# Attention in batches: sums of k on GpSimd, the copy of dilated values ahead of the dilated exponentials, row matmuls behind the other full-array matmuls

## The chip, the cores and the metric

The kernel runs on one core of a Trainium2 chip. The engines are named as in the profile: PE (TensorE, with PEld its weight loads), DVE (VectorE), ACT (ScalarE), POOL (GpSimd) and SP (SyncE, which here issues DMAs). The metric is the device time of one execution in microseconds. The kernel before was timed three times: 841.21, 843.31 and 843.4 us, median 843.31.

## The reference, cut to what matters

Attention over 4 batches, 8 heads, 576 positions and a head dimension of 64 has two branches, which are added. Its result goes through a gated mixture of 8 experts and then through a feed-forward layer. Only attention and the rows handed to the gate are touched here.

```python
q_d = q.reshape(B, H, Sd, factor, D).mean(axis=3)      # factor 4, Sd = 144; k_d, v_d alike
out_d = sm_attn(q_d, k_d, v_d)                          # softmax attention, "dilated"
out_up = np.repeat(out_d, factor, axis=2)
mask = np.abs(pos[:, None] - pos[None, :]) < factor     # local band of 7
scores = np.where(mask, scale * q @ k.T, -1e9)
out_local = softmax(scores) @ v
x = out_up + out_local                                  # rows of 512: 8 heads x 64
logits = x @ w_gate                                     # routing to experts by capacity
...                                                     # experts, then the feed-forward layer
```

## The kernel before, in words

Attention works on 16 pairs of heads (`p`), two heads on the 128 partitions. The local branch of a pair is cut into 9 blocks of 64 positions, and these into three groups of three. Batches `j` of two groups (`BT`, 25 batches) go through a software pipeline. One step of it is called a cycle here: it computes the scores of batch `c` and the transposes and values of batch `c - 2` (`LAG`). A pair has one and a half batches, so three consecutive cycles make a repeating pattern of two pairs.

The steps, with the names that the profile shows:

- Local branch: PE computes the masked scores `sp` (L191, L197). DVE takes their maxima `mxl` (L202) and scales them (L203). ACT computes the exponentials `al`, six a cycle, with their sums `sl` (L210). DVE adds a small number to the sums (L215), takes the reciprocal (L216) and scales `al` (L217). Two cycles later PE transposes `al` into `trl` (L223), ACT copies that to `aT` (L229), and PE multiplies it with v into `pvl` (L240, written pv in the text).
- Dilated branch: POOL adds four neighbouring q into `qdbd` (L106, L109) and four neighbouring v into `v1` (L116, L117; both tiles show as v). DVE adds four neighbouring k into `kd` by one reduction (L121). PE computes the scores `spd` (L136), DVE the maxima `mxd` (L141, L142), ACT the exponentials `ad` (L149), and DVE normalises them (L155 `sd`, L156, L157). PE transposes them into `trd` (L162), DVE copies one half and ACT the other to `adT` (L168), PE multiplies them with `v1` into `opd` (L175), and ACT copies that to `od` (L180).
- DVE adds `pvl` and `od` into `xT` (L254).
- Rows for the gate: PE multiplies a piece of `xT` with an identity beside the gate weights into `rp` (L270, "row matmul"; the two matmuls of one call appear as four instructions in the trace). ACT copies the rows to `xr` (L275), which a DMA stores to DRAM (L286). DVE adds up the gate's part, `lg` (L281) and `L` (L283). There are 36 calls. The first of a cycle uses the one PSUM buffer `rw`; a second one shares the three buffers `tr` with `trl`, `trd` and `opd`.

The order is set by a table of numbers. `emit` gives each step a key, made of the cycle and a fraction; the steps are sorted by key and issued in that order, and `tie` and `pe` keep each engine's queue in the order of issue. Each engine works through its queue in order, so an instruction that waits holds back all behind it. Loads go through SP's queue, sorted the same way. After the last cycle the routing starts, and its first part is already mixed into DVE's queue at the end of attention. The routing's index decides which weights are loaded, and the experts and the feed-forward layer follow.

Of the kernel before, what the change touches and what calls it, by code (L numbers as in the profile page):

```python
# [7 lines left out]
F32 = mybir.dt.float32  # L8
# [6 lines left out]
ALU = mybir.AluOpType  # L15
AX = mybir.AxisListType
# [4 lines left out]
B, H, S, D = 4, 8, 576, 64  # L21
# [9 lines left out]
LAG = 2  # L31
# [23 lines left out]
class Attn:  # L55
# [61 lines left out]
        self.tie('po', G.tensor_tensor(out=v1, in0=v2[:, :, 0], in1=v2[:, :, 1], op=ALU.add))  # L117

    def kdv(self, p):
        kd = self.t[p]['kd'] = self.wk.tile([128, 144], F32, name="kd")  # L120
        self.tie('dv', self.nc.vector.tensor_reduce(out=kd, in_=self.t[p]['k'][:, 3:3 + S].rearrange("p (m r) -> p m r", r=4), op=ALU.add, axis=AX.X))  # L121


    def pe(self, ins):

# [162 lines left out]
    def emit(self, nar=None, rload=None):  # L288
        nc, a = self.nc, self.a
        def masks():  # L290
            nc.sync.dma_start(self.identb, a['identb'])
            nc.sync.dma_start(self.mask.rearrange("p g w -> p (g w)"), a['mask'].rearrange("p g u w -> p (g u w)"))
        def ident():
            nc.sync.dma_start(a['ident_sb'], a['ident'])
        def gate():
            nc.sync.dma_start(a['idg_sb'], a['idg'])
        for i, z in enumerate(self.qdbd):
            (nc.vector if i % 2 == 0 else nc.gpsimd).memset(z, 0.0)
        ops = []
        def add(key, f, *args):  # L300
            ops.append((key, len(ops), f, args))
        nb = len(BT)
        first = lambda p: (3 * p + 1) // 2
        add(-4.7, masks)
        add(-2.5, ident)
        add(1.0, gate)
        add(-4.0, self.busy, FILL0)
        for c, n in FILLC.items():
            add(c + 0.5, self.busy, n)
        for p in range(NP):  # L310
            f = first(p)
            add(1.5 * p - 4.8, self.load, p)
            add(1.5 * p - 2.6, self.load_d, p)
            add(1.5 * p - 1.4, self.load_v, p)
            add(1.5 * p - 2.3, self.prep, p)
            add(1.5 * p + 0.2, self.prep_v, p)
            add(1.5 * p - (1.45 if p != 1 else 0.95), self.kdv, p)
            s = max(f - 1, 0)
            add(s + 0.33, self.spd, p)
            add(s + 0.50, self.mxd, p)  # L320
            add(s + 0.62, self.exd, p)
            add(s + 1.54, self.nmd, p)
            for c in range(2):
                add(s + 2.34 + 0.01 * c, self.trd, p, c)
                add(s + 2.52 + 0.08 * c, self.atd, p, c)
            add(f + LAG + 0.67, self.opd, p)
            add(f + LAG + 1.01, self.odc, p)
        for j in range(nb):
            add(j + 0.00, self.scores, j)
            add(j + 0.04, self.maxes, j)  # L330
            add(j + 0.58, self.exps, j)
            add(j + 1.10, self.norm, j)
            e = j + LAG
            for b in range(len(BT[j])):
                add(e + 0.20 + 0.01 * b, self.trans, j, b)
                add(e + 0.22 + 0.01 * b, self.atc, j, b)
            add(e + 0.70, self.pv, j)
            add(e + 1.02, self.evac, j)
        if rload:
            add(12.0, rload)  # L340
        todo = []
        for t in range(18):
            b, r = divmod(128 * t + 127, S)
            for h in range(2):
                g = 3 * (4 * b + 1 + 2 * h) + r // 192
                k = (g + 1) // 2 + LAG + 1
                todo.append((k + (k < nb + LAG - 1), t, h))
        todo.sort()
        c = 0
        while todo:  # L350
            for n in range(3 if c > nb + LAG - 3 else 2):
                if todo and todo[0][0] <= c and (n == 0 or c % 3 != 1 or c > nb + LAG - 3):
                    _, t, h = todo.pop(0)
                    k = c + (0.30, 0.40, 0.45)[n]
                    if c >= nb + LAG:
                        k = c + 0.04 + 0.1 * n
                    add(k, self.rmm, t, h, n)
                    add(k + (0.15 if c >= nb + LAG - 1 else 0.18 + 0.1 * n), self.rxr, t, h)
                    add(c + 1.06 + 0.01 * n if c < nb + LAG - 1 else k + 0.16, self.rlg, t, h)
                    if h == 1:  # L360
                        add(c + 1.08 if c < nb + LAG - 1 else k + 0.17, self.rst, t)
            c += 1
        for _, _, f, args in sorted(ops):
            f(*args)
# [704 lines left out]
```

## Time and profile before

| | |
|---|---|
| median of three runs | 843.31 us |
| the profiled execution | 837.57 us |
| its span, first to last instruction | 835.8 us |
| busy share of the span: PE, DVE, ACT, POOL | 95%, 80%, 60%, 21% |
| mean granted TensorE clock | 0.995 |

The durations come from the one profiled execution. A busy share is an average over stages that have different limits: attention fills the first 150 us or so, and the experts and the feed-forward layer fill most of the rest. Several instructions that follow each other closely are merged in the timeline, with their count behind an x; the square brackets tell how long the engine had been idle before and what ended that. A wait is put down to the instruction of the other engine that ended last before it.

### The profile page before, as it was taken

The numbers are of one execution on the slowest core, as the hardware profiler recorded it, in microseconds if no ns is written. First come the engines' busy times: TensorE is split into PE (matmuls) and PEld (weight loads), VectorE is DVE, ScalarE is ACT, GpSimd is POOL, SyncE is SP. The second block draws the span as 40 slices with busy tenths as digits, with TensorE's granted clock in tenths as the row PEclk, the third lists the DMA queues.
The fourth block names the chain that finished last, engine by engine and source line by source line (L and its number), as shares of the span: only waits on it lengthen the run. The fifth ranks groups of instructions, "written<-read, shape, count | busy, mean of one in ns | idle before, by whom it ended". The sixth has DMA issues, their size and how long they took to land.

```text
span 835.8 us, 16770 instructions
## 1 busy us (share of the span) xinstructions
PE 795.7 (95%) x6235; PEld 679.2 (81%) x6235; DVE 669.1 (80%) x1699; ACT 497.9 (60%) x1209; POOL 176.0 (21%) x215
## 2 busy tenths in 40 slices
PE   7978888879999999999999999999999999999997
PEld 4877777448998999899998888888878888888886
DVE  6888876768799899999848788888888888657764
ACT  4777777023434444556647777777767777666552
POOL 5654320022121011030000000011223221312223
PEclk9999999999999999999999999999999999999999
DMA  9975532166387496487335434457697674974512
GB/s 240 225 188 180 162 95 102 68 227 223 122 250 253 144 304 238 134 290 276 107 111 183 126 125 128 124 160 199 151 252 175 167 189 103 249 163 128 124 50 76
DMA packets 65106, 142.40 MB, mean 170 GB/s; under 512 B 7968, under 2 KB 20640, under 8 KB 65024
## 3 DMA queue, kind: packets, MB, share of 16 engines
q1 hardware_dynamic: 24704, 70.54, 26.8%
q0 software_dynamic: 29280, 56.63, 26.3%
q10 hardware_dynamic: 11040, 14.16, 4.9%
q8 instruction: 49, 0.80, 0.4%
q14 instruction: 33, 0.27, 0.1%
HBM read 112.98 MB, written 18.88 MB: 158 GB/s over the span
## 4 chain that ended last, share of the span: by engine, by line
PE 66%; issue 8%; DVE 4%; DMA 3%; POOL 2%; ACT 1%; POOLq 0%; SPq 0%; ACTq 0%; DVEq 0%
PE hm L763 6%; PE hm L765 6%; PE hm L764 6%; PE oa L764 6%; PE oa L765 6%; PE oa L763 6%; PE ya L764 4%; PE ya L765 4%; PE ya L763 4%; PE hp L845 4%; PE hp L763 3%; PE hp L764 3%; PE hp L765 3%; PE cnt L522 2%; DMA Yh<-y_dram 1%
## 5 line engine op out<-in xcount | busy, mean ns | idle before, releaser
L763 PE MATMUL hm<-Yh,wM_sb 128*128 128x512 f32 (+1 forms) x320 | 118.5, 370 | 1.6 <-DMA Yh<-y_dram 1.6
L765 PE MATMUL hm<-Yh,wM_sb 128*128 128x512 f32 (+1 forms) x320 | 118.7, 371 | 0.0
L764 PE MATMUL hm<-Yl,wM_sb 128*128 128x512 f32 (+1 forms) x320 | 118.6, 370 | 0.0
L763 PE MATMUL oa<-wM_sb,gh 128*128 128x512 f32 x288 | 113.1, 393 | 0.0
L764 PE MATMUL oa<-wM_sb,gh 128*128 128x512 f32 x288 | 113.1, 393 | 0.0
L765 PE MATMUL oa<-wM_sb,gl 128*128 128x512 f32 x288 | 112.9, 392 | 0.0
L919 DVE SCALAR_TENSOR_TENSOR eu<-eu 128x512 f32<-128x512 f32 x72 | 49.7, 690 | 44.9 <-ACT eu L918 44.6
L763 PE MATMUL ya<-gh,wbh 128*128 128x288 f32 x256 | 79.3, 311 | 1.2 <-DVE Yl L828 1.2
L755 ACT CAST wbh<-wraw 128x512 fp32r<-128x512 f32 x64 | 39.7, 622 | 66.4 <-PE ya L764 37.3
L925 ACT CAST gh<-eu 128x512 fp32r<-128x512 f32 x72 | 44.3, 616 | 54.7 <-DVE eu L922 54.1
L764 PE MATMUL ya<-gl,wbh 128*128 128x288 f32 x256 | 76.4, 299 | 0.2 <-DVE gl L855 0.2
L765 PE MATMUL ya<-gh,wbl 128*128 128x288 f32 x256 | 75.8, 297 | 0.0
L781 POOL DMA_INDIRECT xrow<-x_dram,idx x24 | 32.8, 1366 | 188.8 <-PE ip L623 90.3
L763 PEld LDWEIGHTS hm<-Yh,wM_sb 128*128 128x128 f32 x320 | 60.3, 188 | 13.3 <-DMA Yh<-y_dram 2.3
L926 DVE TENSOR_TENSOR gl<-eu,gh 128x512 fp32r<-128x512 f32 x72 | 49.6, 688 | 25.7 <-ACT gh L925 24.6
L764 PEld LDWEIGHTS hm<-Yl,wM_sb 128*128 128x128 f32 x320 | 60.3, 188 | 11.2
L765 PEld LDWEIGHTS hm<-Yh,wM_sb 128*128 128x128 f32 x320 | 60.2, 188 | 10.7
L914 ACT ACTIVATE eu<-hm 128x512 f32<-128x512 f32 x72 | 42.9, 596 | 40.3 <-PE hm L765 40.1
L763 PEld LDWEIGHTS oa<-wM_sb,gh 128*128 128x128 f32 x288 | 54.0, 188 | 12.8 <-ACT osb L890 0.4
L916 ACT ACTIVATE eu<-eu,one_sb 128x512 f32<-128x512 f32 x72 | 52.1, 724 | 20.6 <-DVE eu L915 19.7
L765 PEld LDWEIGHTS oa<-wM_sb,gl 128*128 128x128 f32 x288 | 54.0, 188 | 12.4
L764 PEld LDWEIGHTS oa<-wM_sb,gh 128*128 128x128 f32 x288 | 54.1, 188 | 11.9
(185 smaller groups left out, 2083.5 us busy)
## 6 DMA issues: line engine op xcount, KB each, us to landing
wraw<-in_wE_dram SPq DMA_DIRECT2D x64, 512.0 KB
n<-in_wM_dram SPq DMA_DIRECT2D x32, 512.0 KB
Yh<-y_dram POOLq DMA_DIRECT2D x16, 1024.0 KB, 9.2
Yl<-y_dram POOLq DMA_DIRECT2D x16, 1024.0 KB, 7.1
part<-osb POOLq DMA_DIRECT2D x36, 256.0 KB, 4.4
vw<-in_vw_dram SPq DMA_DIRECT2D x16, 315.0 KB
kT<-in_kT_dram SPq DMA_DIRECT2D x16, 291.0 KB
qT<-in_qT_dram SPq DMA_DIRECT2D x16, 288.0 KB
```

What stands on the lines that cost most here:

```text
L522: ct = self.behind(nc.tensor.matmul(cnt, cmp[c], OH[:, c], start=(k > 0 and c == 0), stop=(k == 0 and c == 17)))
L755: c = self.nc.scalar.copy(wh, src)
L763: mm(out, lh, rh, start=first, stop=False)
L764: mm(out, lh, rl, start=False, stop=False)
L765: return mm(out, ll, rh, start=False, stop=last)
L781: ld = nc.gpsimd.indirect_dma_start(out=xr, out_offset=None, in_=self.a['x_dram'], in_offset=bass.IndirectOffsetOnAxis(ap=idx[:, g:g + 1], ...
L845: self.r.mm = nc.tensor.matmul(hp, w1[:, 128 * dc:128 * dc + 128], xh[:, dc], start=dc == 0, stop=dc == 3)
L914: nc.scalar.activation(out=e, in_=hp[:, 0:w], func=AF.Exp)
L916: nc.scalar.activation(out=u, in_=e, func=AF.Square, bias=one)
L919: nc.vector.scalar_tensor_tensor(out=u, in0=u, scalar=1.0, in1=r, op0=ALU.add, op1=ALU.mult)
L925: self.cast = nc.scalar.copy(gh[:, 0:w], e)
L926: self.mark = nc.vector.tensor_tensor(out=gl[:, 0:w], in0=e, in1=gh[:, 0:w].bitcast(F32), op=ALU.subtract)
```

## The change

Four things change. The sums of k move from one DVE reduction to two POOL adds, the first over 128x288, the second over 128x144, right behind the q sums of the same pair. The copy `od` is issued with the key of the matmuls that it copies, and the dilated exponentials of all pairs but the first a little later, which puts `od` first on ACT. The copies `adT` of pair 0 are issued earlier. The row matmuls get keys behind `spd` and `trd` and ahead of `opd`, and their copies `xr` keys behind the exponentials.

```diff
--- before.py
+++ after.py
@@ -117,9 +117,12 @@
         self.tie('po', G.tensor_tensor(out=v1, in0=v2[:, :, 0], in1=v2[:, :, 1], op=ALU.add))
 
     def kdv(self, p):
+        G = self.nc.gpsimd
+        k4 = self.t[p]['k'][:, 3:3 + S].rearrange("p (m r) -> p m r", r=4)
+        k2 = self.wk1.tile([128, 144, 2], F32, name="k2")
         kd = self.t[p]['kd'] = self.wk.tile([128, 144], F32, name="kd")
-        self.tie('dv', self.nc.vector.tensor_reduce(out=kd, in_=self.t[p]['k'][:, 3:3 + S].rearrange("p (m r) -> p m r", r=4), op=ALU.add, axis=AX.X))
-
+        self.tie('po', G.tensor_tensor(out=k2, in0=k4[:, :, 0:2], in1=k4[:, :, 2:4], op=ALU.add))
+        self.tie('po', G.tensor_tensor(out=kd, in0=k2[:, :, 0], in1=k2[:, :, 1], op=ALU.add))
 
     def pe(self, ins):
 
@@ -314,17 +317,17 @@
             add(1.5 * p - 1.4, self.load_v, p)
             add(1.5 * p - 2.3, self.prep, p)
             add(1.5 * p + 0.2, self.prep_v, p)
-            add(1.5 * p - (1.45 if p != 1 else 0.95), self.kdv, p)
+            add(1.5 * p - 2.2, self.kdv, p)
             s = max(f - 1, 0)
             add(s + 0.33, self.spd, p)
             add(s + 0.50, self.mxd, p)
-            add(s + 0.62, self.exd, p)
+            add(s + (0.72 if p else 0.62), self.exd, p)
             add(s + 1.54, self.nmd, p)
             for c in range(2):
                 add(s + 2.34 + 0.01 * c, self.trd, p, c)
-                add(s + 2.52 + 0.08 * c, self.atd, p, c)
+                add(s + (2.52 + 0.08 * c if p else 2.36 + 0.08 * c), self.atd, p, c)
             add(f + LAG + 0.67, self.opd, p)
-            add(f + LAG + 1.01, self.odc, p)
+            add(f + LAG + 0.68, self.odc, p)
         for j in range(nb):
             add(j + 0.00, self.scores, j)
             add(j + 0.04, self.maxes, j)
@@ -351,11 +354,11 @@
             for n in range(3 if c > nb + LAG - 3 else 2):
                 if todo and todo[0][0] <= c and (n == 0 or c % 3 != 1 or c > nb + LAG - 3):
                     _, t, h = todo.pop(0)
-                    k = c + (0.30, 0.40, 0.45)[n]
+                    k = c + (0.50, 0.53, 0.56)[n]
                     if c >= nb + LAG:
                         k = c + 0.04 + 0.1 * n
                     add(k, self.rmm, t, h, n)
-                    add(k + (0.15 if c >= nb + LAG - 1 else 0.18 + 0.1 * n), self.rxr, t, h)
+                    add(k + (0.15 if c >= nb + LAG - 1 else 0.10), self.rxr, t, h)
                     add(c + 1.06 + 0.01 * n if c < nb + LAG - 1 else k + 0.16, self.rlg, t, h)
                     if h == 1:
                         add(c + 1.08 if c < nb + LAG - 1 else k + 0.17, self.rst, t)
```

PE's queue, a steady cycle with two row matmuls, from the transposes to the values; before:

```order
L223 MATMUL trl<-ident_sb,al 70x128 x6
L270 MATMUL rp<-idg_sb,xT 128x136 x2
L136 MATMUL spd<-kd,qdbd_154 96x144 x3
L270 MATMUL rp<-idg_sb,xT 128x136 x2
L175 MATMUL opd<-adT,v_1636 64x144 x4
L240 MATMUL pvl<-aT,vw 64x64 x12
```

and now:

```order
L226 MATMUL trl<-ident_sb,al 70x128 x6
L139 MATMUL spd<-kd,qdbd_155 96x144 x3
L273 MATMUL rp<-idg_sb,xT 128x136 x4
L178 MATMUL opd<-adT,v_1350 64x144 x4
L243 MATMUL pvl<-aT,vw 64x64 x12
```

Both calls of the row matmul (two matmuls each) now stand behind `spd`; in cycles with `trd` they stand behind that as well.

ACT's queue, a steady cycle with the copy `adT` and the dilated exponentials; before:

```order
L229 COPY aT<-trl 70x384 x2
L275 COPY xr<-rp 128x256
L210 ACTIVATE al,sl<-sp,mxl 128x70 x6
L168 COPY adT<-trd 72x288
L149 ACTIVATE ad,sd<-spd,mxd 96x144 x3
L180 COPY od<-opd 128x144
```

and now:

```order
L232 COPY aT<-trl 70x384 x2
L213 ACTIVATE al,sl<-sp,mxl 128x70 x6
L171 COPY adT<-trd 72x288
L278 COPY xr<-rp 128x256
L183 COPY od<-opd 128x144
L152 ACTIVATE ad,sd<-spd,mxd 96x144 x3
```

The copy `xr` went from ahead of the six exponentials `al` to behind them and `adT`, and `od` from behind the three exponentials `ad` to ahead of them.

DVE's queue, a steady cycle without `spd`, from the sums `xT` to the copy `adT`; before:

```order
L254 TENSOR_TENSOR xT<-pvl,od 128x192 x2
L202 TENSOR_REDUCE mxl<-sp 128x6
L203 TENSOR_SCALAR mxl<-mxl 128x6
L121 TENSOR_REDUCE kd<-kT 128x144
L281 TENSOR_REDUCE lg<-rp 128x8
L215 TENSOR_SCALAR sl<-sl 128x6
L216 RECIPROCAL sl<-sl 128x6
L217 TENSOR_TENSOR al<-al,sl 128x420
L168 COPY adT<-trd 72x288
```

and now:

```order
L257 TENSOR_TENSOR xT<-pvl,od 128x192 x2
L205 TENSOR_REDUCE mxl<-sp 128x6
L206 TENSOR_SCALAR mxl<-mxl 128x6
L284 TENSOR_REDUCE lg<-rp 128x8
L218 TENSOR_SCALAR sl<-sl 128x6
L219 RECIPROCAL sl<-sl 128x6
L220 TENSOR_TENSOR al<-al,sl 128x420
L171 COPY adT<-trd 72x288
```

The reduction `kd` between the scaled maxima and `lg` is gone; all else stands as it stood. At the end of attention one more thing moves on DVE: the first large compare of the routing, `cmp` (L438), now stands behind the next `xT`, two `lg` and one `sl`. On SP's queue the routing's four tables are issued two pairs of loads later.

## Rows read from the trace of the kernel before

**Rows 1.** Table by stretches, steady part: us, busy per engine (instructions), granted clock, DMA share, GB/s.
```profile
25.79:140.60 114.81, 97.32 (x1595) 86.06 (x1591) 94.11 (x276) 86.14 (x430) 44.88 (x61) 1.00 0.56 163
25.79:34.07 8.28, 8.28 (x154) 7.67 (x150) 7.36 (x19) 6.79 (x35) 5.58 (x7) 1.00 0.91 232
```

**Rows 2.** Waits, 25.79 to 140.6: engine line waited for, us in total, times, longest.
```profile
ACT xr L275 <- PE rp L270: 19.2, 18, 1.7
PE rp L270 <- DVE lg L281: 12.7, 16, 1.5
DVE xT L254 <- ACT od L180: 11.1, 12, 1.8
POOL qdbd L109 <- PE spd L136: 10.4, 6, 2.4
PE rp L270 <- DVE sl L215: 3.4, 2, 1.9
```

**Rows 3.** Timeline of PE, three cycles: start, us long, instruction [idle before it].
```profile
72.32 0.70 PE L270 MATMUL rp<-idg_sb,xT 128*128 128x136 f32 x4 [1.54 <-DVE lg L281]
72.86 0.66 PE L162 MATMUL trd<-ident_sb,ad 96*72 96x96 f32 x6
...
76.96 0.73 PE L270 MATMUL rp<-idg_sb,xT 128*128 128x136 f32 x4 [0.29 <-DVE lg L281]
...
82.96 0.73 PE L270 MATMUL rp<-idg_sb,xT 128*128 128x136 f32 x4 [0.89 <-DVE lg L281]
83.53 0.90 PE L136 MATMUL spd<-kd,qdbd 128*96 128x144 f32 x6
```

**Rows 4.** Timeline of DVE, same cycles.
```profile
71.35 0.74 DVE L121 TENSOR_REDUCE kd<-kT 128x144 f32<-128x576 f32 x1
...
81.47 0.56 DVE L254 TENSOR_TENSOR xT<-pvl,od 128x384 f32<-128x384 f32 x1 [0.95 <-ACT od L180]
```

**Rows 5.** Groups by line, 25.79 to 140.6: shapes xcount, busy us, mean ns, idle before.
```profile
L157 DVE TENSOR_TENSOR ad<-ad,sd 96x432 f32<-96x432 f32 x14 | 10.7, 766 | 0.5
...
L121 DVE TENSOR_REDUCE kd<-kT 128x144 f32<-128x576 f32 x12 | 8.9, 740 | 0.0
...
L203 DVE TENSOR_SCALAR mxl<-mxl 128x6 f32<-128x6 f32 (+1 forms) x21 | 5.5, 260 | 0.7
...
L109 POOL TENSOR_TENSOR qdbd<-q 64x144 f32<-64x144 f32 x22 | 9.5, 432 | 11.5 <-PE spd L136 10.4
...
L106 POOL TENSOR_TENSOR q<-qT 128x288 f32<-128x288 f32 x11 | 8.7, 794 | 0.0
```

**Rows 6.** The scalings of the maxima and of `ad`, 25.79 to 140.6: duration ns min/median/max.
```profile
L203 DVE TENSOR_SCALAR mxl<-mxl x21: 169/172/1027, 27.7 to 137.7; 128x6 f32<-128x6 f32 x20, 128x3 f32<-128x3 f32 x1
...
L157 DVE TENSOR_TENSOR ad<-ad,sd x14: 604/605/1509, 26.1 to 135.3; 96x432 f32<-96x432 f32 x14
```

**Rows 7.** Timeline of POOL and DVE, a v add beside a scaling.
```profile
73.86 1.27 POOL L116 TENSOR_TENSOR v<-vd 72x512 f32<-72x512 f32 x1 [5.18 <-DMA vd<-in_vd_dram]
74.08 1.51 DVE L157 TENSOR_TENSOR ad<-ad,sd 96x432 f32<-96x432 f32 x1
```

**Rows 8.** Timeline of DVE and PE, the first dilated output.
```profile
18.60 0.45 DVE L168 COPY adT<-trd 72x288 f32<-72x288 f32 x1
...
19.19 1.23 PE L175 MATMUL opd<-adT,v 72*64 72x144 f32 x8 [2.61 <-DVE sd L155]
```

**Rows 9.** Table by stretches, 16 to 24 us.
```profile
16.00:20.00 4.00, 1.39 (x15) 1.21 (x15) 3.79 (x10) 3.22 (x19) 3.26 (x5) 0.71 0.95 219
20.00:24.00 4.00, 4.00 (x50) 3.60 (x47) 1.32 (x4) 0.56 (x3) 3.40 (x5) 0.50 0.95 266
```

**Rows 10.** Timeline of DVE and PE, end of attention.
```profile
140.50 1.02 DVE L438 TENSOR_TENSOR cmp<-E,rthr 128x1664 f16<-128x1664 bf16 x1
...
142.12 1.66 PE L270 MATMUL rp<-idg_sb,xT 128*128 128x136 f32 x12 [0.67 <-DVE lg L281]
```

**Rows 11.** Chain that ended last, last gate sum: start, us, what.
```profile
150.53 0.18 DVE L L283
```

## The prediction

> **What bounds the kernel now.** I read the chain of waits first. Attention ends with the last gate sum, at 150.53 us [rows 11]; the chain goes straight on from it into the routing, then the weight loads, the experts and the feed-forward part, all of which need the routing. Nothing later hides a microsecond that attention gives back, so I count gains ahead of 150.53 us one to one.
>
> Then I read the table by stretches for the steady part, 25.79 to 140.60 us [rows 1]. Of 114.81 us PE is busy 97.32, DVE 94.11, ACT 86.14, POOL 44.88. No engine is full, but PE is nearest. The waits of that stretch say what stops it: the row matmuls `rp` wait for DVE's `lg` and, by the order in which DVE ends, `sl`: 12.7 + 3.4 = 16.1 us [rows 2]. PE's whole idle time is 114.81 - 97.32 = 17.5 us, so this one wait is nine tenths of it. `rp` needs the PSUM buffer that `lg` of the cycle before still reads, and `lg` stands on DVE behind `xT`, the maxima and, in some cycles, `kd`. Two more waits belong to it: ACT's `xr` waits 19.2 us for `rp`, with the exponentials queued behind it, and DVE's `xT` waits 11.1 us for ACT's `od`, with `mxl` and `lg` queued behind that.
>
> The timeline shows three consecutive cycles, the pattern that repeats: `rp` waits 1.54, 0.29 and 0.89 us, together 2.72 [rows 3]. In the first, `kd` runs 0.74 us just ahead of `lg`; in the third, `xT` stood 0.95 us for `od` [rows 4].
>
> **The change part by part.** *Row matmuls behind the other full-array work (PE).* In the first kind of cycle `rp` now follows the `trd` transposes (0.66 us), in the second `spd` and `trd` (0.90 + 0.66), in the third `spd` (0.90) [rows 3]. That work fills the time in which `lg` is awaited. In the first cycle 0.66 from the order and 0.74 from the missing `kd` cover 1.40 of 1.54; in the second 1.56 covers 0.29; in the third 0.90 covers 0.89. Left: about 0.14 of 2.72 us. On the PE side the 16.1 us go almost wholly. What is late next is ACT or DVE.
>
> *Copies and exponentials (ACT).* `xr` moves behind the six exponentials, so these no longer stand behind a copy that waits for PE; `od` moves ahead of the three dilated exponentials, so `xT` no longer waits for them. ACT's own work stays at 86.14 us. New: DVE's `sd` now waits for ACT itself, because `od`, for which `xT` waits, no longer comes after `ad`. Behind `sd` stand its reciprocal, the scaling of `ad` and the next `xT`. `ad` now ends behind one or two copies `xr` and the copy `od`, but `sd` comes a cycle after it; I count nothing, and a late `sd` would show as a wait of DVE for `ad`.
>
> *Sums of k (DVE to POOL).* DVE loses 16 reductions of 0.740 us, 11.8 us in all, 8.9 in the stretch. POOL gains 16 pairs of adds. The first has the shape of the q add, 128x288, 0.794 us. The second, 128x144, is not in the trace: its elements per partition are those of `qdbd`, 0.432 us, and it cannot well cost more than the first, 0.794 [rows 5]. I take 0.432, the row with the same length per partition, and keep the other end: 16 x 1.226 = 19.6 us, at most 16 x 1.588 = 25.4. POOL has room: it waits 10.4 us for PE's `spd` before `qdbd` [rows 2], which means that it runs ahead by its three buffers, and in the stretch it is busy 45 of 115 us. Behind the new adds on POOL's queue stand only the v sums and the next q sums. I count no wait of PE for `kd`; if POOL lost its lead, each late pair would cost PE up to the 1.23 us of the two adds.
>
> What it does cost is DVE. Where POOL's `v` add runs from 73.86 for 1.27 us, DVE's scaling of `ad` beside it takes 1.51 us [rows 7], against 0.604 at its fastest; over the stretch its mean is 0.766, and that of the scaling of the maxima 0.260 against a median of 0.172 [rows 5, 6]. So 14 x (0.766 - 0.605) + 21 x (0.260 - 0.172) = 4.1 us of DVE time are lost beside 44.88 us of POOL, 9%. The other small DVE operations lose too; I take double, 18%, an estimate. The stretch gets about 11.5 new pairs, 14 us of POOL, so 2.5 us of new DVE stall. DVE's load there goes from 94.1 to 94.1 - 8.9 + 2.5 = 87.7 us.
>
> The Trainium skill speaks against this part: "SBUF — State Buffer", section "Who interferes with whom", says that VectorE and GpSimd share one port pair as an exclusive lock, that a VectorE instruction with two SBUF inputs blocks against a GpSimd one that reads SBUF, and that a reduction never contends. By it the change swaps a harmless instruction for blocking ones; the trace agrees on the block (1.51 against 0.604 us [rows 6, 7]) and shows it for 9% of the POOL time, 18% by my estimate. By the rule at its worst, all added POOL time stops DVE; that result is the last rival below.
>
> *How much of the 16.1 us comes back.* From 25.79 to 34.07 us no row matmul runs yet. There PE is busy 8.28 of 8.28 us, with DVE at 89%, ACT at 82% and POOL at 67% [rows 1]: this pipeline can run with PE never waiting. After the change DVE wants 87.7 us and ACT 86.1 where PE wants 97.3, so 90% and 88%. For DVE that is what the rows show, for ACT more. If ACT can't pass 82%, the stretch takes 86.14 / 0.82 = 105.1 us, 9.7 saved; if PE sets the pace alone, 16.1 are saved. I take 11.3, three tenths of the waits left, nearer to the end that a row shows.
>
> *Start and end.* The first `opd` waits 2.61 us, and the copies it needs stand behind other work, on DVE at 18.60 us [rows 8]; the diff puts that copy earlier on ACT and `kd` is off DVE's queue. Between 0 and 2.6; I take 0.7, the one `kd`. From 16 to 20 us PE is busy 1.39 us and the granted clock falls to 0.71; from 20 to 24 us PE is fully busy at 0.50, the 1.2 GHz level [rows 9]; if the clock no longer fell, half of those 4 us would come back, which I leave to the range. At the end DVE's first large compare, 1.02 us at 140.50, now stands behind `xT` and two `lg`; behind it today PE's `rp` waits 0.67 us [rows 10]. I take 0.5, between 0 and 0.67. The routing's four small tables load two pairs later on SP's queue; they are used only at the end of attention, so nothing.
>
> **Sum.** 11.3 + 0.7 + 0.5 = 12.5 us. The profiled execution took 837.57 us with a span of 835.8, and should become 825.1. It was 5.7 us below the median of the runs shown, 843.31; on that basis I forecast 830.8 us. Its own range is a gain of 8 to 16 us, 827 to 835.
>
> **The rivals.** *PE sets the pace alone.* For it: the wait-free stretch [rows 1]. Against: ACT at 88% has no row. 16.1 + 2.6 + 0.67, perhaps 2.0 for the clock: 16 to 21 us, about 824. Chance 0.12; the forecast has 0.58.
>
> *ACT takes the place of the wait.* `xr`, `od` and `ad` end later in the cycle, so the next copies `aT` start late and `pv` waits for them. At a share of 79% the stretch takes 109.0 us: 5.8 saved, with start and end 7.0; at 77%, 111.9 us, 2.9 saved, 4.1 with them. Gains of 2.5 to 8 us, so about 838. Chance 0.17. For it: ACT never passed 82%. Against: its waits for `rp`, 19.2 us [rows 2], are what goes.
>
> *The wait only moves,* from `rp` to `trl`, `opd` or `pv`, and nothing is gained: 843. Little speaks for it, since `lg` itself comes earlier. Chance 0.06.
>
> *DVE blocked by POOL: slower.* If POOL's added 19.6 us all stopped DVE, DVE would have 19.6 - 11.8 = 7.8 us more, and with the longer pair 13.6; DVE would then hold `lg` back as it does now and set the pace: 851 us, up to 857. It decides from the point where more than 11.8 / 19.6 = 60% of the added POOL time blocks DVE. The rows show 9 to 18%, and the stretch with POOL at 67% had no PE wait. Chance 0.07. The Trainium skill, "SBUF — State Buffer", section "Who interferes with whom", describes this lock.
>
> **How the numbers follow.** About 0.3%, 2.5 us, is what a measurement of this kernel can tell from no change. Faster: 0.58 + 0.12 + 0.17 = 0.87. Same: 0.06. Slower: 0.07. The range reaches from the rival in which PE sets the pace, 824, to most of the one in which ACT does, 840; beyond it lie the last two and a little at the fast end, under 2 in 10.
>
> **What would show it.** Attention's last gate sum near 138 us instead of 150.53. PE's wait for `lg` under 5 us in the steady part, no wait of ACT's `xr` for `rp`, `xT` no longer waiting for `od`. Means of DVE's scalings above 0.766 and 0.260 while POOL works, and the second add on POOL near 0.43 us. I am wrong if the `rp` wait stays over 8 us, if PE waits as long at `pv` or `trl` instead, or if DVE's scalings lose more than 7 us in all.

## The result and the profile after

The changed kernel took 831.0 us (median of four runs, 825.8 to 833.6) where the kernel before took 842.3 beside it: 0.985 of the time, 95% interval 0.981 to 0.989. That is 11.3 us less; 12.5 were forecast, and 830.8 us. Two later comparisons, on two different chips, gave 826.1 against 842.9 (0.981, 0.978 to 0.984) and 826.6 against 842.6 (0.982, 0.978 to 0.986): gains of 16.8 and 16.0 us. The three intervals overlap, but the later gains are those of the rival "PE sets the pace alone".

The first profiled execution of the changed kernel took 831.68 us with a span of 829.9 us; that of the kernel before took 837.57 us with 835.8. The wait that the change aimed at is gone. Waits of the steady part after, 25.79 to 140.6 us (us in total, times, longest), to be read against [rows 2]:

```profile
...
ACT aT L232 <- PE trl L226: 14.1, 18, 3.2
...
ACT aT L232 <- DMA vd<-in_vd_dram: 5.1, 1, 5.1
DVE mxl L205 <- PE sp L200: 4.4, 9, 1.3
PE trd L165 <- ACT aT L232: 4.2, 3, 2.6
DVE xT L257 <- ACT ad L152: 3.5, 1, 3.5
...
ACT xr L278 <- PE rp L273: 2.6, 4, 1.3
...
PE trd L165 <- DVE lg L284: 2.0, 4, 0.7
DVE xT L257 <- ACT od L183: 1.3, 2, 0.7
...
PE rp L273 <- DVE lg L284: 1.0, 2, 0.5
```

PE's `rp` waits 1.0 us for `lg` instead of 12.7, ACT's `xr` 2.6 instead of 19.2, DVE's `xT` 1.3 for `od` instead of 11.1. What grew is waiting for PE: ACT's `aT` for `trl`, 14.1 us instead of 7.0, and DVE's `mxl` for `sp`, 4.4 instead of 1.0. The three single waits of 5.1, 2.6 and 3.5 us are new; they are one event, below. The timeline of PE shows how `rp` now stands behind `spd` and `trd` (start, us, instruction [idle before it]); compare [rows 3]:

```profile
81.19 0.90 PE L139 MATMUL spd<-kd,qdbd 128*96 128x144 f32 x6
81.92 1.09 PE L273 MATMUL rp<-idg_sb,xT 128*128 128x136 f32 x8
...
86.46 0.69 PE L165 MATMUL trd<-ident_sb,ad 96*72 96x96 f32 x6 [0.29 <-ACT aT L232]
86.99 1.12 PE L273 MATMUL rp<-idg_sb,xT 128*128 128x136 f32 x8
...
91.99 0.69 PE L165 MATMUL trd<-ident_sb,ad 96*72 96x96 f32 x6 [0.48 <-DVE lg L284]
92.51 0.66 PE L273 MATMUL rp<-idg_sb,xT 128*128 128x136 f32 x4
```

No `rp` waits in these three cycles. A little of the wait moved to `trd`, 0.77 us where `rp` had waited 2.72. The table by stretches after (us, then busy us of PE, PEld, DVE, ACT, POOL, the granted clock, DMA share, GB/s), of the whole stretch of [rows 1], of eleven cycles in its second half, and of one cycle ahead of them:

```profile
25.79:140.60 114.81, 105.41 (x1659) 94.04 (x1658) 95.83 (x284) 87.90 (x434) 62.85 (x89) 0.97 0.67 177
74.59:127.19 52.60, 50.72 (x855) 46.24 (x852) 45.16 (x136) 45.04 (x229) 24.95 (x36) 1.00 0.52 152
53.11:63.44 10.33, 7.09 (x86) 6.19 (x83) 6.76 (x16) 5.07 (x26) 8.55 (x14) 0.79 0.90 236
```

From 74.59 us on PE is busy 50.72 of 52.60 us, 96%, with ACT and DVE at 86%. But the one cycle from 53.11 to 63.44 takes 10.33 us, and PE is busy in 7.09 of them although the clock stands at 0.79. The timelines of ACT and of PE there:

```profile
53.16 0.66 ACT L278 COPY xr<-rp 128x256 f32<-128x256 f32 x2
54.63 4.21 ACTq L289 DMA_DIRECT2D x_dram<-xr  x2
58.89 0.85 ACT L232 COPY aT<-trl 70x384 f32<-70x384 f32 x2 [5.07 <-DMA vd<-in_vd_dram]
```

```profile
56.42 0.44 PE L165 MATMUL trd<-ident_sb,ad 96*72 96x96 f32 x3 [0.69 <-DVE lg L284]
59.41 0.70 PE L165 MATMUL trd<-ident_sb,ad 96*72 96x96 f32 x3 [2.56 <-ACT aT L232]
```

ACT's queue takes 4.21 us to issue the first two row stores, until a `vd` load lands, and ACT is idle for 5.07 us; behind the stores stands `aT`, and PE waits for that. Before the change the same two issues took 0.35 and 0.34 us:

```profile
57.49 0.35 ACTq L286 DMA_DIRECT2D x_dram<-xr  x1
...
59.19 0.34 ACTq L286 DMA_DIRECT2D x_dram<-xr  x1
```

PE's idle time is followed by a granted clock of 0.50, the 1.2 GHz level, from 60 to 66 us. The order of the built kernel says why a store waits for a load. In it the transfers of SP and ACT take turns on eight semaphores, DMAHW0 to 7, and each waits until the one before it on its own semaphore is complete. After the change the first two stores have numbers 2 and 4. Eight places ahead of them on these numbers stand a `kT` and a `vd` load, which SP issued at 41.57 and 45.84 us; before, the stores' predecessors were the small tables `rthr` and `rtri`:

```
35 L90 DMA kT_833<-in_kT_dram 128x582 [waits DMAHW2_49]
37 L94 DMA vd_910<-in_vd_dram 72x1024 [waits DMAHW4_49,Pool_49]
...
68 L289 DMA x_dram_57<-xr_780 128x512 [waits DMAHW2_49,Activation_49]
69 L289 DMA x_dram_57<-xr_782 128x512 [waits DMAHW4_49,Activation_49]
```

Attention's last gate sum starts at 140.28 us instead of 150.53 [rows 11], 10.2 us earlier, while the span is 5.9 us shorter:

```profile
140.28 0.17 DVE L286 SCALAR_TENSOR_TENSOR L<-lg 128x8 f32<-128x8 f32 x1
```

What follows attention took 689.6 us, against 685.3 before. Over the fourteen traces of this case it took 684.2 to 690.6, in code that the change doesn't touch.

### The profile page after: what moved, and what is told of

Same layout as the page of the kernel before. It is cut to its first block, busy times and chain, and to the rows that moved or that the text cites. A ratio compares the mean times of both kernels' runs of the same rounds, so it can differ in the third digit from the quotient of the medians.

```text
span 829.9 us, 16780 instructions
## 1 busy us (share of the span) xinstructions
PE 798.7 (96%) x6235; PEld 682.1 (82%) x6235; DVE 666.5 (80%) x1683; ACT 495.9 (60%) x1209; POOL 195.6 (24%) x247
## 4 chain that ended last, share of the span: by engine, by line
PE 73%; DMA 11%; issue 8%; DVE 4%; POOL 2%; ACT 1%; SPq 0%; POOLq 0%; ACTq 0%; DVEq 0%
PE hm L768 7%; PE hm L767 7%; PE hm L766 7%; PE oa L766 6%; PE oa L767 6%; PE oa L768 6%; DMA vd<-in_vd_dram 5%; PE ya L767 4%; PE ya L768 4%; PE ya L766 4%; PE hp L848 3%; PE hp L766 3%; PE hp L768 3%; PE hp L767 3%; PE cnt L525 2%
## 5 line engine op out<-in xcount | busy, mean ns | idle before, releaser
L922 DVE SCALAR_TENSOR_TENSOR eu<-eu 128x512 f32<-128x512 f32 x72 | 49.7, 690 | 45.0 <-ACT eu L921 44.7
L767 PEld LDWEIGHTS hm<-Yl,wM_sb 128*128 128x128 f32 x320 | 60.6, 189 | 11.3
L894 POOL DMA_DIRECT2D part<-osb x36 | 33.2, 1014 | 138.0 <-ACT osb L893 112.0
L766 PEld LDWEIGHTS oa<-wM_sb,gh 128*128 128x128 f32 x288 | 54.1, 188 | 12.8 <-ACT osb L893 0.4
```

What stands on the lines that cost most here:

```text
L766: mm(out, lh, rh, start=first, stop=False)
L767: mm(out, lh, rl, start=False, stop=False)
L894: nc.gpsimd.dma_start(p, o, accum_op=ALU.add)
L922: nc.vector.scalar_tensor_tensor(out=u, in0=u, scalar=1.0, in1=r, op0=ALU.add, op1=ALU.mult)
```

## The experiments

All ran beside the kernel before, in three comparisons; the numbers are medians of six runs, those of the kernel before of eleven. Each kernel has one trace, and the last three columns come from it. One measure is used throughout, from the timeline of PE: how long nine cycles take, from the start of the 5th cycle's scores to the 14th's (first half, where the changed kernel's loads keep the DMA engines about 90% busy) and from the 14th's to the 23rd's (second half).

| kernel | ratio to before, 95% | first half, us | second half, us | last gate sum, us |
|---|---|---|---|---|
| before | 1 | 49.0 | 51.1 | 150.5 |
| changed, three traces | 0.985, 0.981, 0.982 | 50.6, 44.1, 44.9 | 43.6, 43.6, 45.2 | 140.3, 134.5, 135.8 |
| row matmuls alone | 0.991 (0.988 to 0.994) | 46.7 | 46.0 | 141.1 |
| copies alone | 0.992 (0.989 to 0.994) | 50.0 | 48.7 | 148.0 |
| sums of k alone | 0.993 (0.990 to 0.995) | 49.9 | 49.7 | 150.0 |
| without sums of k | 0.986 (0.983 to 0.989) | 47.1 | 44.9 | 137.6 |
| tables early | 0.980 (0.978 to 0.983) | 47.1 | 44.2 | 136.1 |
| tables early, without sums of k | 0.983 (0.980 to 0.986) | 45.7 | 45.4 | 136.7 |
| sums of k doubled | 0.986 (0.983 to 0.988) | 45.0 | 45.3 | 141.9 |
| late stores | 0.982 (0.978 to 0.986) | 43.7 | 46.0 | 136.7 |
| first three sums on DVE | 0.980 (0.976 to 0.984) | 43.7 | 43.8 | 133.8 |
| both | 0.982 (0.978 to 0.986) | 44.7 | 46.7 | 138.3 |

In each of the three single parts the routing's tables move as well, though no edit names them: SP issues `rthr` at 60.60, 66.58 and 55.40 us in the traces of the row matmuls, the copies and the sums, and at 44.23 in the kernel before. None of the three is its part alone, then. What the later tables do in the kernel before was not tried; in the changed kernel, early tables leave the time as it is (below).

**Row matmuls alone.** The kernel before with

```
-                    k = c + (0.30, 0.40, 0.45)[n]
+                    k = c + (0.50, 0.53, 0.56)[n]
-                    add(k + (0.15 if ... else 0.18 + 0.1 * n), self.rxr, t, h)
+                    add(k + (0.15 if ... else 0.10), self.rxr, t, h)
```

> The kernel before with only the row matmuls and their copies xr moved to the end of the full-array part; kd stays on DVE, od stays behind the dilated exponentials. Theory (all three parts cure one and the same wait, PE's rp behind DVE's lg, 16.1 us, so alone each gives less than its share and the three together less than their sum would be): by the rows of the three cycles the moved work fills 0.66 + 0.29 + 0.90 = 1.85 of 2.72 us, 68%, so 11 us of the wait at most, less what DVE then still loses to kd and od: a gain of 6 to 9 us against before, PE's wait for lg down to 4 to 8 us, DVE's xT still waiting about 10 us for ACT's od. Rival (the row matmuls do everything): a gain of 10 to 13 us, the same as the whole change. Rival (without kd and od moved, xT only becomes later and the wait moves to trl or pv): a gain of 0 to 2 us.

Measured: 833.5 against 841.1 us, 7.6 less. Waits, 25.79 to 140.6 us:

```profile
...
DVE xT L254 <- ACT od L180: 7.6, 11, 1.6
PE rp L270 <- DVE lg L281: 4.9, 8, 1.0
...
ACT xr L275 <- PE rp L270: 2.5, 4, 1.3
```

The theory's gain and its wait for `lg` hold; `xT` waited 7.6 us for `od` rather than about 10. By the last gate sum, one trace of each kernel, this part brings 9.5 us, where the whole change brings 10.2, 16.0 and 14.7 in its three traces, the copies 2.5 and the sums 0.5. By the medians the three parts are not told apart (7.6, 6.6 and 5.5 us), and together they are more than the whole.

**Copies alone.** The kernel before with

```
-            add(s + 0.62, self.exd, p)
+            add(s + (0.72 if p else 0.62), self.exd, p)
-            add(f + LAG + 1.01, self.odc, p)
+            add(f + LAG + 0.68, self.odc, p)
```

and the first pair's `adT` copies earlier, as in the change.

> The kernel before with only od moved ahead of the dilated exponentials (and the first pair's dilated copies earlier). Theory: xT's wait for od, 11.1 us in the steady part, goes; lg stands behind xT, so lg comes earlier in the cycles in which od was waited for, one in three or so with 0.95 us, and PE's wait for lg falls by 3 to 5 us; a gain of 3 to 5 us. Rival (the row matmuls do everything): 0 to 1 us. Rival (od ahead of ad makes ad late, sd waits): 0 to 3 us slower, with DVE waiting for ad at sd.

Measured: 834.5 us, 6.6 less; more than expected by the medians. The trace bears out half of the reason:

```profile
...
ACT xr L275 <- PE rp L270: 14.1, 17, 1.7
...
PE rp L270 <- DVE lg L281: 11.9, 18, 1.7
...
DVE xT L254 <- ACT od L180: 1.4, 2, 0.8
```

`xT` hardly waits for `od` any more, but PE still waits 11.9 us for `lg` where a fall by 3 to 5 was expected; the last gate sum is only 2.5 us earlier. Part of that is a hold-up in this trace too: ACT is idle 2.80 and 2.74 us at row stores, and the cycle from 62.05 takes 7.9 us.

```profile
59.80 0.85 ACT L229 COPY aT<-trl 70x384 f32<-70x384 f32 x2 [2.80 <-PE spd L136]
...
67.01 0.85 ACT L229 COPY aT<-trl 70x384 f32<-70x384 f32 x2 [2.74 <-PE rp L270]
```

The traced execution of the kernel before was 3.5 to 5.3 us below the medians of that kernel, so a trace set against it shows less than the medians do, and where the rest of the 6.6 us lies isn't shown.

**Sums of k alone.** The kernel before with the new `kdv` and its key.

> The kernel before with only the sums of k moved to GpSimd. Theory: kd, 0.74 us, no longer stands ahead of lg in two of three cycles; in the stretch that is 8.9 us less DVE work, of which about half stands in the time in which PE waits: a gain of 3 to 6 us, POOL busy 19.6 us more, means of DVE's scalings up by under 0.1 us. Rival (DVE blocked by GpSimd): no gain or up to 5 us slower, with the scalings' means up by 0.2 us or more. Rival (the row matmuls do everything): 0 to 1 us.

Measured: 835.5 us, 5.5 less, with the same reserve; the last gate sum is 0.5 us earlier.

```profile
...
DVE xT L257 <- ACT od L183: 13.4, 13, 1.8
PE rp L273 <- DVE lg L284: 12.8, 16, 1.5
```

In the trace the missing reductions only let DVE wait longer for `od`, 13.4 instead of 11.1 us, and PE waits for `lg` as before; where the 5.5 us of the medians lie, it doesn't show. GpSimd did not slow the kernel.

**Without the sums of k.** The changed kernel with the old `kdv` and its key.

> The changed kernel with the sums of k back on DVE at their old place in the order. Theory: with the row matmuls behind spd and trd, PE waits little for lg even with kd on DVE, but DVE's load returns to about 94 us in a stretch of 105, nearly full, so 2 to 5 us slower than the changed kernel, still 6 to 10 us faster than before; DVE busy over 92% in the steady part. Rival (GpSimd's adds cost DVE more than the reduction did): up to 3 us faster than the changed kernel. Rival (kd is off every path): within 1 us of the changed kernel. The hold-up of ACT's queue at the first row stores, 4.2 us in the changed kernel, should be there in this one too, since the routing tables stand equally late on SP's queue.

Measured: 828.3 against 841.1 us, 12.8 less; from this comparison alone, no different from the changed kernel. The hold-up of ACT's queue, expected here too, did not come: the two issues took 0.83 us, not 4.2. DVE was busy 46.4 of 52 us from 70 us on, 89%, not over 92. The next comparison, with the changed kernel in it, is the better test of the sums.

**The changed kernel again.** No edit.

> The changed kernel once more, unaltered, as the measure for the next three and for a second trace. Theory (ACT's queue stands at the issue of the first two row stores, because each of them waits for the completion of an older load that is still under way, and behind it stand aT, xr and ad): the hold-up appears again near 54 us, for 3 to 5 us, one cycle of the scores lasts 9 to 11 us, and the granted clock falls to 0.50 behind it; 829 to 832 us. Rival (the hold-up of the first trace was an accident of one execution, not of the order): all cycles from 25 to 120 us under 6.5 us, time nearer to 826.

Measured: 826.1 against 842.9 us. In this execution the rival holds: no cycle from 25 to 120 us is over 6.3 us. Line of ACT's queue at the first two stores, then its table row from 73.97 to 123 us:

```profile
52.96 0.83 ACTq L289 DMA_DIRECT2D x_dram<-xr  x2
```

```profile
73.97:123.00 49.03, 47.23 (x795) 43.02 (x791) 42.01 (x133) 42.03 (x214) 20.04 (x27) 1.00 0.46 138
```

The 0.83 us are the two issues one behind the other, and ACT's next copy then waits for PE. So the hold-up is not in every execution: the issues took 4.21, 0.83 and, in a third trace, 2.36 us. The order makes it possible; that the speed of the loads ahead decides it fits the first trace, where the `vd` load lands 12.7 us after its issue, but was not tried. Without it the first half takes 44.1 us instead of 50.6.

**Tables early.** The changed kernel with

```
-            add(12.0, rload)
+            add(8.0, rload)
```

> The changed kernel with the routing's four small tables loaded earlier (before the seventh pair's v rows instead of after the tenth pair's k), nothing else. The first two row stores then wait for small tables that landed long before, instead of a k load and a v load just issued. Theory (the store's wait holds ACT): the issue at the first stores takes under 1 us, no cycle over 7 us there, the clock stays at 1.00 from 25 us on; attention's last gate sum 3 to 5 us earlier than in the changed kernel; 3 to 6 us faster than it, about 826. Rival (the loads themselves set the pace up to 65 us, and the store only shows it): the late cycle stays, with aT or v1 or qdbd waiting for a load, and the time within 1.5 us of the changed kernel.

Measured: 826.1 us, the same as the changed kernel in that comparison; the trace still has a cycle of 9.1 us, from 50.30. ACT stands 5.0 us ahead of `aT`, and the profile's view of the table `rthr` names `aT` as what waited for it.

```profile
56.03 0.85 ACT L232 COPY aT<-trl 70x384 f32<-70x384 f32 x2 [5.01 <-issue]
```

The tables `rsmall` and `rthr`, which stand ahead of the two stores on their semaphores here, were issued at 44.82 and 46.43 us and had not landed when the stores came near 51; SP had issued its vd load just ahead at 43.06, into DMA engines that are 91% busy from 25 to 50 us. So my edit had exchanged one late predecessor for another, and the premise "landed long before" was false.

**Tables early, without the sums of k.** The last edit and that of the variant without the sums, together.

> The changed kernel with the tables earlier and with the sums of k back on DVE. Theory (the store's wait accounts for what the sums of k seemed to cost): since the variant without the sums on GpSimd had a hold-up of only 0.83 us, earlier tables give it under 1.5 us; with the tables early, the sums on GpSimd are worth 0 to 3 us, so this one is 0 to 3 us slower than the changed kernel with early tables. Rival (GpSimd's adds cost DVE more than the reduction did): this one is the fastest of all, 2 us or more faster than the changed kernel with early tables.

Measured: 828.7 us, 2.5 more than with the sums on GpSimd in the same comparison. That is as the theory has it (0 to 3), against the rival, and at the edge of what can be told apart.

**Sums of k doubled.** The changed kernel with each add issued twice:

```
-        self.tie('po', G.tensor_tensor(out=k2, ...))
+        for _ in range(2):
+            self.tie('po', G.tensor_tensor(out=k2, ...))
```

and the same for `kd`.

> The changed kernel with each of the two adds of k issued twice on GpSimd (the same result written twice): POOL's work up by another 17.4 us (16 times 0.665 + 0.425). Theory (a tenth to a fifth of POOL's time stops DVE, and DVE has room): 1.7 to 3.5 us more DVE time, of which under half shows, 0 to 2 us slower than the changed kernel; means of DVE's scalings up by less than 0.1 us. Rival (POOL's time blocks DVE one to one): 8 us slower or more, DVE busy over 95% of the steady part. A second rival is POOL's own lead: up to about 55 us POOL is busy three quarters of the time, and with 1.1 us more for each pair PE waits there at spd for kd, 3 to 6 us in all.

Measured: 830.6 us, 4.5 more than the changed kernel. The cycles take no longer (45.0 and 45.3 us); the loss is at the start, where the second rival put it, though before 24 us rather than up to 55:

```profile
18.94 1.75 PE L141 MATMUL spd<-kd,qdbd 128*96 128x144 f32 x6 [3.01 <-POOL kd L127]
```

The fourth cycle's scores start at 23.61 us, in the changed kernel of the same comparison at 19.17. Summed over DVE's groups up to the last gate sum, DVE was busy 125.2 us, against 123.1, 121.5 and 118.5 in the three traces of the changed kernel: 4.2 us more than their mean, for 19.9 us more of POOL, 21%. The three traces differ among themselves by 4.6 us, so the share is rough; but POOL does not block DVE one to one.

**Once more, and three variants.** The last comparison was about the two losses seen.

> The changed kernel, unaltered, as the measure for the next three. Theory (in the steady part PE alone sets the pace; now and then an execution loses 4 to 5 us near 54 us where ACT's queue stands at a row store behind a load that lands late): 825 to 831 us, 12 to 17 us less than before. Rival (the first comparison, 11.3 us, is the typical one): 830 to 833 us.

Measured: 826.6 against 842.6 us. The first two stores took 2.36 us, but the larger loss came later, at the fourth store:

```profile
64.60 0.85 ACT L232 COPY aT<-trl 70x384 f32<-70x384 f32 x2 [1.92 <-DMA kT<-in_kT_dram]
```

ACT was idle 1.92 us until a `kT` load landed, PE waited 2.23 us at `trd`, the granted clock was 0.50 from 66 to 72 us, and the cycles from 60.42 and 68.43 took 8.0 and 6.9 us.

Late stores:

```
-                        add(c + 1.08 if c < nb + LAG - 1 else k + 0.17, self.rst, t)
+                        add(min(c + 4.08, nb + LAG + 0.08) if c < nb + LAG - 1 else k + 0.17, self.rst, t)
```

with the stores tied into ACT's order. In this order the tables `rthr` and `rtri` stand ahead of the first two stores again, as in the kernel before, so both the time of the stores and what they wait for have changed.

> The changed kernel with the row stores of the steady part three cycles later in ACT's order, near 68 us and after, where the loads are through; nothing else. Theory (the store's wait on an older transfer holds ACT only while the load queue is full): no hold-up of ACT's queue over 1.5 us between 50 and 70 us, no cycle over 7 us there, and the spread of the times smaller; the median 0 to 3 us below the changed kernel's in the same comparison. Rival (the loads themselves set the pace there): a cycle of 8 us or more stays, with another wait for a load, and the time is within 1 us.

```profile
67.01 0.35 ACTq L289 DMA_DIRECT2D x_dram<-xr  x1
67.46 0.40 ACTq L289 DMA_DIRECT2D x_dram<-xr  x1
```

In this trace there is no hold-up and no cycle between 50 and 70 us is over 5.3 us, with the same loads under way. That speaks for the store as what held ACT and against the rival (the loads set the pace); but the changed kernel's second trace had no hold-up either, and the last variant below, with the same late stores, had one. And the time, 828.3 us, is not below the changed kernel's 826.6. The first half is the shortest with one other, 43.7 us; the second half, 46.0, is longer than in the changed kernel. Why isn't settled.

The first three sums of k on DVE, with their old keys:

```
+        if p < 3:
+            kd = ...; self.tie('dv', self.nc.vector.tensor_reduce(out=kd, ...)); return
```

> The changed kernel with the sums of k of the first three pairs on DVE again, at their old place; the other thirteen stay on GpSimd. Theory (at the start GpSimd has no lead, and PE waits 1.2 to 1.9 us at spd for its kd): that wait falls to 1.0 us or less, the fourth cycle of the scores starts 0.5 to 1.5 us earlier unless the granted clock falls otherwise; 0 to 2 us faster than the changed kernel. Rival (DVE is the engine at its limit at the start): opd waits again 1 to 2.6 us for DVE, as before the change, and the time is the same or up to 1.5 us more.

Measured: 825.1 us, the lowest median of all, 1.5 below the changed kernel beside it and inside the scatter of either (822.0 to 828.9 and 822.3 to 830.2). PE no longer waits for `kd` at the start, but `opd` waits 1.5 us for DVE's `adT`: theory and rival each hold for one wait, and the fourth cycle starts no earlier (19.47 us; 19.89, 19.17 and 19.19 in the changed kernel).

> The changed kernel with both: row stores three cycles later and the first three sums of k on DVE. Theory: the two act in different places, so their gains add: 0 to 5 us below the changed kernel in the same comparison, 824 to 826 us if both hold. Rival: no measurable difference from the changed kernel, within 1.5 us.

Measured: 828.2 us, 1.6 us more than the changed kernel beside it and inside the scatter; the gains of the theory are not there. Its first two stores, at 71 us, were held again, this time behind the table `rtri`, which SP had issued at 65.09 us; ACT was idle 3.3 us, and the cycle from 68.14 took 6.8 us (line of the waits: us in total, times, longest):

```profile
ACT aT L236 <- DMA rtri<-in_rtri_dram: 3.3, 1, 3.3
```

No version is shown to beat the changed kernel.

## Why the prediction was right, and where not

The time, 830.8, was met at first and lies 4.7 and 4.2 us above the later two medians; the direction and the place, the `rp` wait and the last gate sum (near 138; 140.3, 134.5 and 135.8), were right. By its steps:

- **Row matmuls behind `spd` and `trd`: right.** [rows 3] left about 0.14 of 2.72 us by the sum; `rp` waits none and `trd` 0.77 in three cycles after. The row matmuls alone gave 7.6 us by medians.
- **How much of the 16.1 us comes back: the term that was mis-sized.** I left three tenths, because ACT had no row above 82%. After, PE is busy 96% with ACT and DVE at 86%: the bound read from one stretch of 8.28 us [rows 1] was no bound. From the 5th cycle to the last gate sum the traces took 124.7 us before, and 109.9 in the execution without a hold-up: 14.9 less, nine tenths of the 16.1. In the first, 116.3, 8.5 less. That the first comparison met the forecast is luck: the 11.3 us that I took lie between these two; the pipeline does better than I gave it, and in the first execution it lost about 6.5 us in its first half again.
- **The tables on SP's queue, "nothing": failed.** Their move changed what the first row stores wait for, and in the first trace ACT was idle 5.07 us by it. I had looked at when the tables are used, not at what their place in the count of semaphores does. How much of the difference between 11.3 and 16.8 us it explains isn't settled: moving the tables did not lower the time, nor did the stores' later place, and both moves still had a hold-up in a trace (5.0 and 3.3 us) when what the store waited for had not landed.
- **`od` ahead of `ad`: right as a whole.** `xT`'s wait for `od` went from 11.1 to 1.3 us; it waited once, 3.5 us, for `ad` in the held-up cycle, and not at all in the other two traces. No wait for a late `sd` shows.
- **Sums of k: the costs right.** POOL's busy time rose from 176.0 to 195.6 us, the 19.6 forecast. The second add was put near 0.43 us, and DVE's scalings were to go above 0.766 and 0.260 [rows 5]:

```profile
L124 POOL TENSOR_TENSOR k<-kT 128x288 f32<-128x288 f32 x12 | 8.6, 713 | 0.9
L125 POOL TENSOR_TENSOR kd<-k 128x144 f32<-128x144 f32 x12 | 5.8, 484 | 0.9
```

```profile
L160 DVE TENSOR_TENSOR ad<-ad,sd 96x432 f32<-96x432 f32 x14 | 10.9, 780 | 0.5
...
L206 DVE TENSOR_SCALAR mxl<-mxl 128x6 f32<-128x6 f32 (+1 forms) x21 | 6.0, 285 | 0.7
```

  (Groups after: busy us, mean ns, idle before.) The share of POOL's time that stops DVE, put at 18%: with the sums alone DVE's busy time to the last gate sum is 120.5 us, where 127.3 less 16 x 0.740 would be 115.5, so 5.0 of 19.6 us or 26%; in the changed kernel against the two without the sums it is 16%, doubled 21%. These shares are rough: traces with the same work on DVE differ by 2.6 us in this sum (127.3 before, 128.5 with the row matmuls alone, 129.9 with the copies alone) and those of the changed kernel by 4.6. All lie far from the 60% at which the slower rival would begin. The 3.1 to 5.0 us that DVE lost beside 19.6 us of POOL fit the lock that the Trainium skill describes ("SBUF — State Buffer", section "Who interferes with whom").
- **The start: right size, other reasons.** I took 0.7 us and no wait for `kd`. The 5th cycle starts 1.8, 1.2 and 2.2 us earlier in the three traces. PE's first `opd` waits 0.39 us instead of 2.61 [rows 8], but `spd` waits 1.9 us for POOL, 1.0 for DVE's `kd` before, where I had POOL ahead:

```profile
16.26 0.98 PE L139 MATMUL spd<-kd,qdbd 128*96 128x144 f32 x6 [1.38 <-POOL kd L125]
...
18.12 1.19 PE L178 MATMUL opd<-adT,v 72*64 72x144 f32 x8 [0.39 <-DVE adT L171]
```

  POOL's wait for PE [rows 2] was read from the steady part; in the first three pairs POOL has no lead yet, which doubling its work made plain.
- **The end: right, and given back.** The 0.67 us behind `cmp` [rows 10] are gone. But from the last gate sum to the first expert matmul it takes 28.0 to 28.9 us in all eleven traces with the row matmuls moved, and 27.4 in the three without. The traces show where: from the last gate sum to the first gather of rows (`xrow`) all fourteen take 19.0 to 19.1 us, but in the chain of waits the piece that waits for the gather to land is 3.06 to 3.09 us long in the three and 3.85 to 4.72 in the eleven. Before and after (start, us, what):

```profile
173.51 3.06 DMA xrow<-x_dram,idx
```

```profile
163.30 4.39 DMA xrow<-x_dram,idx
```

  Why the gather lands later was not tried.
- **Microseconds ahead of the last gate sum count one to one: only in the mean.** The rest of the kernel varies by 6 us among traces, which no experiment here controls.

## What to carry to other kernels

Where an engine waits for a buffer, look for work of its own that can stand in that time; here the reordering of one engine took the wait from 12.7 to 4.9 us by itself, and moving work off the engine waited for left it at 12.8. An engine's share in one short stretch is no upper bound for what it can do. Whoever moves a transfer in a program whose transfers share semaphores in turn should list, for each transfer issued from a computing engine, which older transfer it will wait for.

## What the runs showed that was not expected

- A store that waits on ACT's queue for an older load left ACT idle for 5.07 us in one execution of the changed kernel, for 2.16, 0.91 and 1.92 us at three places in another, and not at all in a third. Small tables held stores too: one issued at 46.43 us still held a store near 54 us, and one issued at 65.09 a store near 71 us.
- PE reached 96% beside two engines at 86%.
- The clock's fall at the start comes and goes. In the first trace of the changed kernel PE is busy 0.88 and 1.47 of 2 us from 14 to 18 us, and the granted clock is 0.55 from 18 to 20; with early tables PE is busy 1.53, 1.32 and 1.60 of 2 us from 14 to 20 us, and the clock stays at 1.00 up to 24 us. What decides it isn't shown.
